# The second half of each spectrum swap, issued from ScalarE's queue

## The chip, the cores and the metric

One core of a Trainium2 chip. The metric is the device time of one execution in microseconds (us). The program uses the core's five instruction queues: TensorE (PE), VectorE (DVE), ScalarE (ACT), GpSimd (POOL) and SyncE (SP). Here SP only issues transfers (DMAs). POOL does little (iotas, memsets and seven accumulating transfers).

## What is computed

Two long convolutions over a sequence of 2048 steps and 448 channels, and a gated sum of them:

```python
g = sigmoid((x * gate_w).sum(-1, keepdims=True))   # x = A_u
a = A(x)            # kernel K[d,l] = Re sum_n C exp(dt A l) dt B, from 448 x 256 complex modes
b = B(x, k, v)      # kv = (4-tap causal conv of k) * v ; kernel ssm_k ; then times x
out = g * a + (1 - g) * b
```

Each branch is a causal convolution written as irfft(rfft(padded input) * rfft(padded kernel)) in length 4096, plus a skip term. Branch A must first make its 2048-tap kernel K from the modes.

## The kernel before

**Tiling.** The FFTs are matmuls with sine tables. The 448 channels are cut into NQG = 4 groups of 112 (4 x 28 columns). For each group H and branch, three spectra-like tiles of 128 partitions x 3584 bf16 are made in two steps: `spread` (L328, matmuls with Wc, PSUM tile ps_c) and `transform` (L340, matmuls with the table s_W, PSUM tile ps_2, shown as ps). Both are brought from PSUM to SBUF by `evac` (L728), which is a copy on ACT: in the profile "CAST zs<-ps_c" and "CAST zs<-ps" (zsK for the kernel of branch A). The tile is changed in place.

**Swap and product.** A complex product needs, beside a spectrum zs, the same spectrum with its upper and lower 64 partitions exchanged (real and imaginary parts). `swapped` (L764) makes that copy, zsS, with two transfers of 64 partitions x 3584 bf16 (448 KB each) from SBUF to SBUF. There are eight swaps: KB[0] at L852, KB[1] to KB[3] at L975, XA[0] to XA[2] at L977 and XA[3] at L1006. `products` (L399) then multiplies zsS and zs in place by the other spectrum on DVE, 2.0 us each; for XA[3], `last` (L1008) does it in quarters. Multiplying zs in place overwrites what the swap reads, so either multiply needs the swap to be through. Next `stage_a` (L374) makes ps_a from both on PE, ACT copies it to U, and `stage_b` (L387) makes ps_b.

**Work woven in between.** In `block` (L891, and KGen.block, L464), DVE builds products of exponentials for branch A's kernel (tiles kg_TQ, kg_TP, kg_P), PE multiplies them (pk, then ps_g) and ACT copies the results (kg_S, kg_KT). The tables come from `Tables.levels`: DVE makes phases (ks_ph), ACT takes sines and exponentials of them (ET, ks_mag), DVE multiplies these. ACT needs an ACT_TABLE_LOAD of 1.28 us when it changes between sine and exponential.

**Order.** Nothing runs in the order of the source. `Order` (L137) records all 6779 calls of the five engines in one list and issues them in the order of ORDER (L42), a fixed list of call numbers. Within an engine every instruction gets a dependency on the one before, so each queue runs exactly in the list's order. The two calls of a swap have neighbouring numbers (729 and 730 the first in time, 5009 and 5010 the seventh), and stand somewhere ahead of the multiply in ORDER. In the list, that is a place between calls for all engines; what it means for a queue depends on which other calls that queue holds. The line of every instruction in the profile is L149, inside `issue`, so tiles tell instructions apart. The tiles zs, zsS, U and others share six buffers (NBQ, L39).

```python
    dmae = [nc.sync, nc.scalar]
    ...
    def store(b0, n):
        for g in range(4):
            dmae[g % 2].dma_start(out4[g][:, b0:b0 + n, :], ug[g * 32:(g + 1) * 32, b0:b0 + n, :])
```

`dmae` (L714) exists already: the output is stored from SP and ACT in turn. ACT's other transfers are five small ones at the start (ldt and shift_k).

Of the kernel before, what the change touches and what calls it, by code (L numbers as in the profile page):

```python
# [690 lines left out]
def body(  # L691
# [20 lines left out]
    nc = Order(tc)  # L712
    V = nc.vector
    dmae = [nc.sync, nc.scalar]  # L714
# [25 lines left out]
    def qt(shape, name, dtype=bf16):  # L740
        return qp.tile(shape, dtype, name=name, tag="q")
# [22 lines left out]
    def swapped(zs):  # L764
        swap = qt([P, 32, 4 * NC], "zsS")
        for r in range(2):
            nc.sync.dma_start(swap[64 * r:64 * r + 64], zs[64 - 64 * r:128 - 64 * r])
        return zs, swap

    early = kgp.tile([P, 7168], i32, name="early", tag="kg_TQ")  # L770
# [79 lines left out]
    def kv_cols(H):  # L850
        return lambda c: vt[:, :, H * NC + c]
    KB[0] = swapped(KB[0])  # L852
    XB[0] = spread_in(kv_cols(0))
    transform(nc, psum, W2, XB[0], evac)
# [100 lines left out]
    def step(c, n, j):  # L955
        kind, H = n or (None, None)
        if kind == "B":
            KB[H] = spread_in(skc.pop(H))
            XB[H] = spread_in(kv_cols(H))
        elif kind == "A":  # L960
            XA[H] = spread_in(u_cols(H))
        if c:
            U = stage_a(nc, psum, qp, R, terms[c], evac)
        if kind == "B":
            transform(nc, psum, W2, KB[H], evac)
            transform(nc, psum, W2, XB[H], evac)
        elif kind == "A":
            transform(nc, psum, W2, XA[H], evac)
        if c:
            stage_b(nc, psum, G, U, epilogue(*c))  # L970
        if kind == "B" and H + 1 < NQG:
            skc[H + 1] = sk_cols(H + 1)
        block(j)
        if kind == "B":
            terms[n] = products(nc, *swapped(KB[H]), XB[H])  # L975
        elif kind == "A":
            XA[H] = swapped(XA[H])  # L977
            transform(nc, psum, W2, KA[H], evac)
            terms[n] = products(nc, *XA[H], KA[H])
# [81 lines left out]
```

## Time and profile before

| | |
|---|---|
| runs, us | 264.91, 266.36, 268.63 |
| median, us | 266.36 |
| profiled execution, us | 266.88 |
| its span, first to last instruction, us | 264.8 |
| mean granted TensorE clock | 0.942 |
| swap transfers | 16, all on SP, 448 KB each, median 4.4 us from issue to landing |
| duration of a swap's issue on SP, us | 0.46 to 2.22, median 0.56 |

Times in the profile are microseconds from the span's start. A row of a timeline is start, duration, engine, line, operation, tile written <- tiles read, shapes and count; in brackets, how long the engine had been idle and what ended that. SPq and ACTq are transfers being issued by those queues; their data arrive later ("landing"). A row of waits is who waited for whom: us in total, times, longest.

### The profile page before, as it was taken

How to read it: one execution, taken by the hardware profiler on the slowest of the kernel's cores; microseconds unless marked ns; L12 is line 12 of the kernel's file. 1: busy time of each engine (PE TensorE's matmuls, PEld its weight loads, DVE VectorE, ACT ScalarE, POOL GpSimd, SP SyncE). 2: the span in 40 equal slices, each digit the busy share in tenths (PEclk: the TensorE clock that was granted, in tenths of full speed). 3: DMA queues.
4: the chain of work that ended last, by engine and by line, in shares of the span. 5: the costliest groups of instructions: out<-in, count | busy, mean ns of one | idle time of the engine just before them, and what ended most of it. 6: DMA issues, size and time to landing. Idle time of an engine off the chain costs nothing.

```text
span 264.8 us, 12775 instructions
## 1 busy us (share of the span) xinstructions
PE 213.7 (81%) x5786; PEld 194.2 (73%) x5786; DVE 243.4 (92%) x506; ACT 226.8 (86%) x375; POOL 11.8 (4%) x46
## 2 busy tenths in 40 slices
PE   1611849799799999999899898899979998989820
PEld 1501739788688889889788788889969888979720
DVE  6599999899999999999989999989999999989950
ACT  2998789997999999999999999999999999485400
POOL 8000000000000100010100100001000100000000
PEclk9999979999999869999999999999986999999955
DMA  7999669952833702045626230423240360600087
GB/s 153 218 189 192 104 134 203 176 83 32 158 72 72 159 4 57 4 80 119 109 51 141 41 92 2 90 56 73 50 97 2 72 144 2 144 5 2 2 158 122
DMA packets 57077, 24.27 MB, mean 92 GB/s; under 512 B 52032, under 2 KB 54720, under 8 KB 57024
## 3 DMA queue, kind: packets, MB, share of 16 engines
q1 hardware_dynamic: 50752, 19.34, 38.9%
q0 software_dynamic: 1008, 3.21, 6.6%
q10 hardware_dynamic: 5264, 0.92, 2.1%
q8 instruction: 45, 0.74, 1.2%
q14 instruction: 8, 0.07, 0.1%
HBM read 7.95 MB, written 2.87 MB: 41 GB/s over the span
## 4 chain that ended last, share of the span: by engine, by line
DVE 37%; ACT 35%; PE 16%; DMA 4%; issue 3%; SPq 0%; ACTq 0%; DVEq 0%
ACT zs L149 12%; ACT zsK L149 7%; ACT ET L149 6%; DVE kg_P L149 5%; PE ps_v L149 4%; ACT U L149 4%; DVE kg_TQ L149 3%; PE ps_b L149 3%; DVE kg_TP L149 3%; DVE ET L149 3%; PE ps_c L149 3%; DVE zsS L149 3%; DVE vt L149 3%; DVE zs L149 3%; DVE sb_G L149 2%
## 5 line engine op out<-in xcount | busy, mean ns | idle before, releaser
L149 ACT CAST zs<-ps 128x896 bf16<-128x896 f32 x48 | 43.8, 944 | 1.9 <-PE ps L149 1.9
L149 ACT CAST zs<-ps_c 128x1024 bf16<-128x1024 f32 (+1 forms) x48 | 44.0, 976 | 0.5 <-PE ps_c L149 0.4
L149 PEld LDWEIGHTS <-front 128*32 128x32 bf16 (+1 forms) x496 | 19.9, 160 | 27.8 <-issue 17.3
L149 PE MATMUL pk<-kg_TP,kg_TQ 128*32 128x32 bf16 x1792 | 35.4, 241 | 0.9 <-issue 0.7
L149 PEld LDWEIGHTS <-kg_TQ 128*32 128x32 bf16 x1792 | 31.8, 160 | 3.5 <-issue 0.9
L149 PEld LDWEIGHTS <-s_W 128*128 128x128 bf16 x544 | 27.9, 98 | 7.9 <-issue 4.5
L149 PE MATMUL ps_a<-sa_R,zs 128*128 128x128 bf16 x224 | 32.0, 231 | 1.2 <-DVE zs L149 0.7
L149 PE MATMUL ps_b<-U,sb_G 128*128 128x28 bf16 x1024 | 30.8, 178 | 2.6 <-DVE U L149 1.2
L149 ACT CAST U<-ps_a 128x1024 bf16<-128x1024 f32 (+1 forms) x30 | 27.9, 962 | 5.4 <-PE ps_a L149 5.4
L149 PEld LDWEIGHTS <-sb_G 128*128 128x128 bf16 x1024 | 28.7, 98 | 4.7 <-issue 1.9
L149 PE MATMUL ps_v<-front 128*32 128x336 bf16 (+3 forms) x448 | 17.3, 319 | 17.1 <-DVE sb_offs L149 6.9
L149 PE MATMUL ps_a<-sa_R,zsS 128*128 128x128 bf16 x224 | 31.1, 227 | 0.0
L149 PEld LDWEIGHTS <-zs 128*128 128x128 bf16 x224 | 29.0, 150 | 1.9 <-DVE zs L149 0.8
L149 PEld LDWEIGHTS <-zsS 128*128 128x128 bf16 x224 | 29.4, 152 | 0.7 <-DVE zsS L149 0.4
L149 PE MATMUL ps<-zs,s_W 128*128 128x112 bf16 x384 | 27.1, 215 | 3.0 <-ACT zs L149 2.5
L149 DVE TENSOR_TENSOR kg_TP<-kg_TP,ET 128x1792 bf16<-128x1792 bf16 x23 | 24.7, 1083 | 0.5 <-ACT ET L149 0.5
L149 DVE TENSOR_TENSOR kg_TQ<-kg_TQ,ET 128x896 bf16<-128x896 bf16 (+1 forms) x36 | 24.6, 720 | 0.0
L149 ACT ACTIVATE ET<-ks_ph 128x448 bf16<-128x448 int16 x40 | 22.6, 596 | 1.8 <-DVE ks_ph L149 1.7
L149 DVE TENSOR_TENSOR kg_P<-kg_TP,ET 128x1792 bf16<-128x1792 bf16 (+1 forms) x25 | 23.3, 934 | 0.1
L149 ACT ACT_TABLE_LOAD x15 | 19.2, 1283 | 2.0 <-issue 1.8
L149 PE MATMUL ps_c<-Wc,uu 128*64 128x128 bf16 x224 | 18.7, 290 | 0.4 <-ACT zsK L149 0.2
L149 PE MATMUL ps_c<-Wc,vt 128*64 128x128 bf16 x224 | 17.2, 289 | 1.2 <-ACT zs L149 1.2
(101 smaller groups left out, 424.7 us busy)
## 6 DMA issues: line engine op xcount, KB each, us to landing
zsS<-zs SPq DMA_DIRECT2D x16, 448.0 KB, 4.4
kg_TP<-kg_P POOLq DMA_DIRECT2D x7, 448.0 KB, 4.4
vt<-in_B_v_dram SPq DMA_DIRECT2D x4, 448.0 KB, 7.5
skraw<-in_B_ssm_k_dram SPq DMA_DIRECT2D x16, 112.0 KB, 3.4
uu<-in_A_u_dram SPq DMA_DIRECT2D x4, 448.0 KB, 7.1
ks_xf<-xfd SPq DMA_DIRECT2D x3, 336.0 KB, 3.1
out_dram<-vt SPq DMA_DIRECT2D x8, 112.0 KB, 4.4
out_dram<-vt ACTq DMA_DIRECT2D x8, 112.0 KB, 4.6
```

What stands on the lines that cost most here:

```text
L149: ins = f(*args, **kw)
```

## The change

`swapped` issues its first transfer (r = 0) on SP as before and its second (r = 1) on ACT. The transfers' contents, sizes and places in ORDER stay the same.

```diff
     def swapped(zs):
         swap = qt([P, 32, 4 * NC], "zsS")
         for r in range(2):
-            nc.sync.dma_start(swap[64 * r:64 * r + 64], zs[64 - 64 * r:128 - 64 * r])
+            dmae[r].dma_start(swap[64 * r:64 * r + 64], zs[64 - 64 * r:128 - 64 * r])
         return zs, swap
```

In the built program the orders on PE, DVE and POOL are unchanged. SP loses eight transfers. ACT gains them, each at the place that its number has in ORDER among ACT's own calls:

| swap | spectrum | on ACT behind | and ahead of |
|---|---|---|---|
| 1 | KB[0] | cast zs<-ps of 66.9 us | cast zs<-ps_c of 67.67 |
| 2 | KB[1] | exponential ET<-ks_xf of 91.49 | cast zs<-ps_c of 92.00 |
| 3 | KB[2] | cast zs<-ps of 129.0 | sine ET<-ks_ph of 129.83 |
| 4 | XA[0] | exponential ET<-ks_xf of 146.5 | exponential of 146.8 |
| 5 | XA[1] | cast zs<-ps of 178.7 | sine ET<-ks_ph of 179.47 |
| 6 | KB[3] | exponential ET<-ks_xf of 199.68 | exponential of 199.97 |
| 7 | XA[2] | copy kg_KT<-ps_g of 224.09 | cast zs<-ps of 224.52 |
| 8 | XA[3] | cast zsK<-ps of 237.34 | cast zsK<-ps of 237.8 |

The times are the starts of those instructions in the trace of before.

## The prediction

> **What bounds the kernel now.** I read the page's busy lines, then the table by stretches, VectorE's (DVE) waits, and the timelines of SP, ScalarE (ACT) and DVE around each swap.
>
> ```profile
> PE 213.7 (81%) x5786; PEld 194.2 (73%) x5786; DVE 243.4 (92%) x506; ACT 226.8 (86%) x375; POOL 11.8 (4%) x46
> ```
> ```profile
> 91.50:129.00 37.50, 35.98 (x1000) 32.48 (x1003) 37.03 (x68) 36.94 (x67) 0.86 (x1) 0.92 0.33 64
> 129.00:149.00 20.00, 18.00 (x582) 16.46 (x584) 18.80 (x41) 19.32 (x37) 0.86 (x1) 1.00 0.35 74
> 149.00:178.50 29.50, 27.62 (x736) 25.24 (x730) 28.66 (x54) 29.47 (x52) 0.85 (x1) 1.00 0.29 62
> 178.50:198.60 20.10, 18.44 (x538) 16.67 (x537) 20.01 (x48) 20.07 (x34) 0.86 (x1) 0.95 0.34 73
> 198.60:220.70 22.10, 21.71 (x570) 20.10 (x568) 21.08 (x30) 21.66 (x38) 0.85 (x1) 0.89 0.31 65
> 220.70:237.90 17.20, 15.60 (x581) 14.20 (x580) 16.24 (x17) 12.54 (x20) 0.00 (x0) 1.00 0.25 57
> ```
> The columns are the stretch, its length, then busy time of PE, weight loads, DVE, ACT, POOL. From 91.5 to 237.9 us DVE idles 0.47+1.20+0.84+0.09+1.02+0.96 = 4.6 us out of 146.4, and ACT is full until 220. Two in-order engines without slack hand work to each other: a DVE stall is hardly ever absorbed.
>
> DVE's waits, longest first:
> ```profile
> DVE front L149 <- DMA scratch<-in_B_shift_k_dram: 3.1, 1, 3.1
> DVE ks_ph L149 <- ACT ET L149: 1.9, 2, 1.1
> ...
> DVE zsS L149 <- ACT zsK L149: 0.6, 2, 0.4
> ```
> Only the start-up wait is for a DMA. No multiply ever waits for a swap: all sixteen swap transfers are hidden, so landing them sooner buys nothing.
>
> The place where I expect most, on SP, ACT and DVE:
> ```profile
> 212.28 1.10 SPq L149 DMA_DIRECT2D zsS<-zs  x2
> ```
> ```profile
> 222.65 0.53 ACT L149 CAST kg_S<-pk 128x448 bf16<-128x448 f32 x1
> 223.14 0.91 ACT L149 CAST zs<-ps 128x896 bf16<-128x896 f32 x1
> 224.09 0.53 ACT L149 CAST kg_KT<-ps_g 128x448 bf16<-128x448 f32 x1
> 224.52 0.91 ACT L149 CAST zs<-ps 128x896 bf16<-128x896 f32 x1
> ```
> ```profile
> 220.76 2.02 DVE L149 TENSOR_TENSOR zsS<-zsS,zsK 128x3584 bf16<-128x3584 bf16 x1 [0.39 <-ACT zsK L149]
> ```
> SP issues both halves at 212.28, far ahead of the multiply at 220.76. In the changed kernel's own order the second half stands on ACT behind the kg_KT copy of 224.09 and ahead of the cast of 224.52: after the multiply that needs it.
>
> Does ACT's queue reach a transfer early? The start-up is the one spot with a DMA behind an ACT instruction that waits:
> ```profile
> 4.42 0.20 ACT L149 ACTIVATE scratch<-ldt 112x4 bf16<-112x4 bf16 x1 [1.36 <-DMA ldt<-in_A_log_dt_dram]
> 4.43 1.35 ACTq L149 DMA_DIRECT2D scratch<-in_B_shift_k_dram  x3
> ```
> The first of these three transfers waits for nothing, yet goes out 0.01 us after the ACTIVATE ahead gets its data. It does not wait for that ACTIVATE's end (4.62), but it does not overtake its wait either. So a transfer on ACT leaves when the last ACT instruction ahead of it has what it waits for.
>
> **Landing price.** Swap issues land after 4.0/4.4/6.7 us (least, median, most; the tile view of zsS). The late ones are second halves queued behind their first; one issued alone, as here, should be near the short end: 4.2 us, between 4.0 and 4.4; 6.7 is the far bound.
>
> **Part 1: eight second halves leave SP.** SP is rid of 8 x 0.56 us (median issue) and of some waits; it idles for most of the span, and the skraw and ks_xf loads behind it move up 0.6 us but nobody waits for them. Worth 0. A faster landing is worth 0 too, as above.
>
> **Part 2: ACT's time.** Issues on ACT's queue cost 0.42 (ldt) to 0.56 us. Behind a 0.9 us cast they are hidden, since the queue works while the engine does; behind the 0.39, 0.53 and 0.55 us instructions of the second, seventh and eighth swap some 0.1 to 0.2 us shows, and there ACT will soon be waiting for DVE anyway. I take 0; the bounds are 0 and 8 x 0.56 = 4.5 us.
>
> **Part 3: the added wait on DVE.** A multiply needs both halves: zsS is written by them, and zs may not be overwritten until both were read. Per swap: the ACT row ahead of the transfer, that time + 4.2, the multiply's start now, and the difference.
> - First: cast at 66.9 (second of the pair 66.09 to 67.81), lands 71.1; multiply 72.94. On time, 0.
> - Second: ET exponential at 91.49, kept until then by the table load of 90.20 + 1.28; lands 95.7; multiply 91.74. **4.0 late.**
> - Third: cast at 129.0 (second of 128.06 to 129.93), 133.2; multiply 129.78. **3.4.**
> - Fourth: between 144.64 (a table load ends and six exponentials and casts can be queued) and 146.5 (the last of them starts); lands 148.8 to 150.7; multiply 149.12: -0.3 to 1.6. I take **0.5**, as little behind that table load waits for anybody.
> - Fifth: cast at 178.7, 182.9; multiply 178.52. **4.4.**
> - Sixth: cast at 198.89 (the exponential behind it waits for nothing), 203.1; multiply 198.59. **4.5.**
> - Seventh: 224.09, 228.3; multiply 220.76. **7.5.**
> - Eighth: zsK cast at 237.34, 241.5; multiply 237.90. **3.6.**
>
> Sum 27.9 us. Behind each stalled multiply the whole DVE queue waits: ks_ph phases that ACT turns into ET tables, kg_TP/kg_TQ that PE multiplies, the products that PE's ps_a needs. So ACT becomes late as well, and with it the next swap's transfer; that is why the stalls add. Two things are taken off. DVE's own idle time of 4.6 us can absorb lateness once. And where ACT has a lead over DVE it is less late at the next transfer: after the second swap the exponentials at 98.34 use a kg_TP sum that ended at 97.16, a lead of 1.2, of which the idle time already counts 0.3: 0.9. Elsewhere the lead is nearly nil: the PE waits for "DVE zs" at 224.78, right behind the product. Net 27.9 - 4.6 - 0.9 = **22.4 us**.
>
> The profiled execution took 266.88 us (span 264.8 and 2.1 around it; the median of the runs is 266.36). 266.9 + 22.4 = 289.3; I say **289 us**.
>
> Bounds: least, if lateness never reached ACT, so that stalls did not add: the largest alone, 7.5, gives 274. Most: nothing absorbed and every issue paid, 27.9 + 4.5 gives 299. The value is nearer the upper end, as ACT and DVE are both full.
>
> [...]
>
> **Rivals.**
> 1. *ACT's queue overtakes (not slower).* If a transfer on ACT passed instructions that still wait, it would leave as soon as its own data and buffer are there, which is when SP issues it now: 212.28 + 0.5 for the seventh swap, not 224.09. All seven would be on time as today: 266.9. It decides only if such passing happens, against which the rows at 4.42 and 4.43 speak. [...] The start-up rows show a transfer held back with a single waiting instruction ahead.
> 2. *Stalls do not add up.* ACT keeps going while DVE waits, so each transfer leaves near its old time and DVE's lateness covers the next stall: 274 to 280. For it: ACT's table work has leads of about 1 us here and there. Against: ACT's full rows and its many waits for DVE and, through PE, for products.
> 3. *More than counted.* Landings take 6.7 us as the slowest now do: seven late swaps x 2.5 us more, 266.9 + 22.4 + 17.5 = 307. Against: nothing is queued ahead of a half that leaves 10 us after the other.
> 4. *The swap truly gets faster.* Both halves leave together and DVE gains: at most 8 x 0.56 = 4.5 us, 262. Against: no multiply waits for a swap today.
>
> **How the numbers follow.** Forecast with adding stalls 0.83; rival 1, 0.04; rival 2, 0.06; rival 3, 0.06; rival 4, 0.01. The likeliest is 289. If ACT found its lead of 1.2 again behind each of the five late swaps that follow the second (6.0) and all landings took 4.0 (7 x 0.2), the sum would be 15.0 and the time 281.9; the range starts at 280, the edge of rival 2, and ends at 299, the bound with every issue paid and nothing absorbed. It leaves out under 2 in 10. About 2% is what a measurement of this kernel tells from no change: faster 0.01, within 2% 0.04, slower 0.95.
>
> **What would show it.** DVE's waits should have new entries, zs and zsS waiting for the DMA zsS<-zs, seven of them and over 20 us in all, the longest about 7 us at the seventh swap. Issues should read eight on SPq and eight on ACTq, the latter just behind the ACT rows named, landing in 4.0 to 4.4 us. DVE's busy time should stay at 243 us and its share fall to about 84%. PE should run the same 5786 matmuls with more gaps, ps_a's above all. I am wrong if ACTq's swap issues come earlier than the ACT instruction ahead gets its data, or if ACT is found on time at each next transfer although DVE was late.

## The result and the profile after

| | before | changed |
|---|---|---|
| median, us | 266.07 | 296.0 |
| range, us (4 runs each) | 264.91 to 268.63 | 295.28 to 296.6 |
| profiled execution, us (span) | 266.88 (264.8) | 295.92 (294.1) |
| mean granted TensorE clock in it | 0.942 | 0.913 |

The ratio is 1.110, 95% interval 1.105 to 1.114: slower by 11%, 30 us. The forecast was 289, from 280 to 299.

The busy line of the changed kernel's page; each entry is busy time, share of the span and count:

```profile
PE 220.0 (75%) x5786; PEld 199.8 (68%) x5786; DVE 243.7 (83%) x506; ACT 227.8 (77%) x375; POOL 11.8 (4%) x46
```

DVE and ACT do the same work in about the same busy time as before (243.4 and 226.8 us then). PE needs 220.0 us instead of 213.7 for the same 5786 matmuls, at the lower granted clock of the table above. For DVE, the 29 us are waiting. Who makes DVE wait, longest first (us in total, times, longest):

```profile
DVE zsS L149 <- DMA zsS<-zs: 12.4, 3, 7.8
DVE zsS L149 <- PE ps L149: 4.6, 1, 4.6
DVE zs L149 <- DMA zsS<-zs: 4.4, 1, 4.4
DVE zs L149 <- ACT kg_S L149: 4.1, 1, 4.1
DVE zsS L149 <- ACT uu L149: 3.9, 1, 3.9
...
DVE kg_KT L149 <- PE ps_g L149: 2.2, 1, 2.2
...
DVE ks_ph L149 <- ACT ET L149: 0.2, 1, 0.2
```

Before, not one of these waits was for a swap. Now the five upper rows, 29.4 us over seven multiplies, are. Three of them name PE or ACT as the releaser, which is the profile's guess among several semaphores: those multiplies (191.17, 137.85 and 215.06 us) start 4.0 to 4.9 us after an ACT issue of a swap; of the four that name the DMA, three do so 4.0 to 4.1 us after one, and the multiply at 96.39 starts 6.2 us after.

The seventh swap in the changed kernel, on SP's queue, on ACT and its queue, then on DVE:

```profile
228.74 0.46 SPq L149 DMA_DIRECT2D zsS<-zs  x1
```
```profile
239.62 0.91 ACT L149 CAST zs<-ps 128x896 bf16<-128x896 f32 x1
240.57 0.53 ACT L149 CAST kg_KT<-ps_g 128x448 bf16<-128x448 f32 x1
240.63 0.47 ACTq L149 DMA_DIRECT2D zsS<-zs  x1
241.14 0.91 ACT L149 CAST zs<-ps 128x896 bf16<-128x896 f32 x1
```
```profile
244.61 2.03 DVE L149 TENSOR_TENSOR zsS<-zsS,zsK 128x3584 bf16<-128x3584 bf16 x1 [7.76 <-DMA zsS<-zs]
```

SP issued the first half at 228.74. The second leaves 0.06 us after the kg_KT copy ahead of it starts, 11.9 us later, and the multiply begins 4.0 us after that. ACT itself loses nothing: the next cast follows at 241.14.

### The profile page after: what moved, and what is told of

Its sections match the earlier page's. It is cut to its first block, busy times and chain, and to the rows that moved or that the text cites. A ratio compares the mean times of both kernels' runs of the same rounds, so it can differ in the third digit from the quotient of the medians.

```text
span 294.1 us, 12780 instructions
## 1 busy us (share of the span) xinstructions
PE 220.0 (75%) x5786; PEld 199.8 (68%) x5786; DVE 243.7 (83%) x506; ACT 227.8 (77%) x375; POOL 11.8 (4%) x46
## 3 DMA queue, kind: packets, MB, share of 16 engines
q1 hardware_dynamic: 50112, 15.67, 29.7%
## 5 line engine op out<-in xcount | busy, mean ns | idle before, releaser
L149 PE MATMUL ps_a<-sa_R,zs 128*128 128x128 bf16 x224 | 37.2, 254 | 18.7 <-DVE zs L149 18.1
L149 PEld LDWEIGHTS <-zs 128*128 128x128 bf16 x224 | 31.1, 154 | 19.7 <-DVE zs L149 18.7
L149 ACT CAST zs<-ps_c 128x1024 bf16<-128x1024 f32 (+1 forms) x48 | 43.3, 957 | 0.3 <-PE ps_c L149 0.3
L149 ACT CAST U<-ps_a 128x1024 bf16<-128x1024 f32 (+1 forms) x30 | 27.1, 929 | 20.4 <-PE ps_a L149 20.3
L149 PEld LDWEIGHTS <-front 128*32 128x32 bf16 (+1 forms) x496 | 20.9, 158 | 26.6 <-issue 15.8
L149 PE MATMUL ps_a<-sa_R,zsS 128*128 128x128 bf16 x224 | 36.4, 251 | 2.0 <-DVE zsS L149 2.0
L149 PEld LDWEIGHTS <-zsS 128*128 128x128 bf16 x224 | 31.5, 155 | 3.0 <-DVE zsS L149 2.6
L149 PE MATMUL ps_v<-front 128*32 128x224 bf16 (+3 forms) x448 | 18.5, 335 | 15.7 <-DVE front L149 6.9
L149 DVE TENSOR_TENSOR zsS<-zsS,zsK 128x896 bf16<-128x896 bf16 (+1 forms) x7 | 8.5, 1223 | 17.0 <-DMA zsS<-zs 12.4
```

What stands on the lines that cost most here:

```text
L149: ins = f(*args, **kw)
```

## The experiments

Two theories. *Place*: a transfer on ACT leaves when ACT's queue has come to its place in the list; DVE's stalls are the whole loss, and they add. Rival, *queue*: an issue from ACT, or a second queue of transfers, costs by itself wherever it stands. A second question is what makes the loss larger than forecast. Each run was timed against the kernel before on the same chip (267.16 us in the first four, 266.94 in the last three).

**1. The same queue, an earlier place.** Eight numbers of ORDER moved; all else as changed (in short, as the list itself is one long string):

```diff
-ORDER: second halves 730, 1833, 3306, 2455, 3928, 5854, 5010, 5954 at their old places
+ORDER: 730 behind 1346, 1833 behind 2902, 3306 behind 4173, 2455 behind 3419,
+       3928 behind 2875, 5854 behind 5459, 5010 behind 5503, 5954 behind 5219
```

> All eight second halves stay on ACT, but each stands earlier in the list, right behind the first ACT call that starts 0.2 us or more after SP's issue of that swap in the trace of before (65.17, 84.59, 123.24, 141.75, 168.57, 190.11, 212.59, 226.06 us). Theory place (a transfer on ACT leaves when ACT's queue has come to its place, and the stalls of DVE are all of the loss): it leaves about as early as SP's half, lands before every multiply, DVE waits for no swap; 266 to 268 us. Rival queue (issuing from ACT costs by itself: ACT's time, or two queues that get into each other's way): the same eight issues, so still about 290 us or more.

Measured: 269.9 us, ratio 1.0105 (1.0055 to 1.0154). DVE's waits:

```profile
DVE front L152 <- DMA scratch<-in_B_shift_k_dram: 3.4, 1, 3.4
DVE ks_ph L152 <- ACT ET L152: 3.2, 2, 2.1
...
DVE kg_TP L152 <- ACT ET L152: 1.0, 1, 1.0
```

No swap is waited for any more, so 26 of the 30 us are gone with the same eight issues on ACT. The time lies 2 us above what I expected. DVE waits longer for ET tables than before (3.2 + 1.0 against 1.9 + 0.5 us), and ACT now has eight issues of about 0.47 us in its queue. That these are the cause is not shown: in the trace of run 2, where ACT issues no swap, the ks_ph wait is 2.9 us as well. The cause of these 2 us stays open. The run bounds what issuing on ACT costs: 1%, not 11%.

**2. A queue with little in it, the old place.**

```diff
-            dmae[r].dma_start(swap[64 * r:64 * r + 64], zs[64 - 64 * r:128 - 64 * r])
+            [nc.sync, nc.gpsimd][r].dma_start(swap[64 * r:64 * r + 64], zs[64 - 64 * r:128 - 64 * r])
```

> The list is as in the changed kernel, but the second half goes out on POOL's queue, which holds only seven accumulating transfers besides. Theory place: what stands ahead on POOL is done early, so the swap leaves in time although its number stands at the same late place of the list; 266 to 269 us. Rival queue, in the form that transfers from two queues slow each other: 285 us or more. If POOL's issue itself took long, landings would be 1 to 2 us later than from SP, which the multiplies can bear.

Measured: 267.58 us, ratio 1.0025 (0.9999 to 1.005): the same as before. POOL's first half left at 65.0 us and its last at 226.4; SP's left at 64.5 and 226.1. So on this queue the late place in the list cost nothing, and neither did a second queue of transfers (267.58 against 267.16 us). Nor did it bring the pair home sooner when both halves left close together: in this run the halves of both queues landed 4.0 to 7.6 us after their issue (median 5.7; before, 4.0 to 6.7, median 4.4), and ACT's in run 1 after 5.1 to 6.5 (median 6.2), where the second halves on SP's queue before took 5.7 to 6.7. So even at a good place the second queue shortened no swap. With run 1 this settles *place*: it takes ACT's full queue and the late place together.

**3. Only the seventh swap on ACT.** `swapped` counts its calls (in the source's order, XA[2] is the sixth) and uses ACT in that one alone (shortened):

```diff
+        count.append(1)
         for r in range(2):
-            dmae[r].dma_start(...)
+            dmae[r * (len(count) in (6,))].dma_start(...)
```

> Only the seventh swap (XA[2]) has its second half on ACT. Theory place: one stall of about 7.5 us at its multiply, 0.4 to 1 of it absorbed by DVE's own idle time and some more given back through a longer kg_KT wait as in the changed kernel; 272 to 276 us, middle 274. Rival queue: an eighth of the loss of 30, so 270 us; the stall at the seventh multiply would not be 7 us.

Measured: 275.4 us, ratio 1.0332 (1.0279 to 1.0385): 8.2 us from one transfer.

```profile
DVE zsS L149 <- DMA zsS<-zs: 7.8, 1, 7.8
...
DVE kg_KT L149 <- PE ps_g L149: 2.2, 1, 2.2
```

The stall is the 7.8 us of the changed kernel, and the longer kg_KT wait comes with it (0.6 before).

**4. Both halves on ACT.**

```diff
-            dmae[r].dma_start(...)
+            nc.scalar.dma_start(...)
```

> Both halves of every swap go out on ACT, at their places in the list. Theory place: the departure is as in the changed kernel, but now two transfers queue behind each other, and the pair is complete 5.7 to 6.7 us after the first issue, not 4.0; at seven swaps with a stall that is 1.7 to 2.5 us each on top, since nothing absorbs it: 296 + 12 to 18 = 308 to 314 us. Rival queue: the loss per ACT issue doubles, 296 + 30 = 326 us.

Measured: 310.07 us, ratio 1.162 (1.157 to 1.167), within 308 to 314 and far from 326. DVE's waits for swaps have grown to 24.3 + 13.3 us, and 4.6 more under PE's name. Doubling ACT's issues did not double the loss; the first halves too now stand in ACT's queue (sixteen issues, from 66.9 to 276.9 us), and landings take up to 7.7 us, where the changed kernel's take up to 6.7.

**5. Only the second swap on ACT** (`in (2,)` in the edit of run 3), 200 us of program behind it:

> Only the second swap (KB[1]) has its second half on ACT: one stall of about 4.4 us at its multiply, with the whole rest of the program behind it to make up for it. Theory absorption (as my prediction had it: DVE's 4.6 us of idle time take up lateness once): nearly all is made up, 266 to 268 us. Theory pass-through (most of that idle time is DVE waiting for ACT or PE, which are late as well, so little is made up; in the changed kernel only 0.3 and 1.1 of the idle rows that follow went away): 1.5 made up, 269.5 to 271 us.

Measured: 270.48 us, ratio 1.0126 (1.0094 to 1.0159): *pass-through*. The multiply and DVE's largest waits:

```profile
95.90 2.03 DVE L149 TENSOR_TENSOR zs<-zs 128x3584 bf16<-128x3584 bf16 x1 [4.25 <-DMA zsS<-zs]
```
```profile
DVE zs L149 <- DMA zsS<-zs: 4.2, 1, 4.2
DVE front L149 <- DMA scratch<-in_B_shift_k_dram: 3.3, 1, 3.3
DVE ks_ph L149 <- ACT ET L149: 1.9, 2, 1.1
```

The ks_ph waits for ACT stay at 1.9 us, as before: ACT was late by as much as DVE, so this idle time absorbed nothing. All of DVE's idle rows over 0.15 us from the first swap on, other than the stall, sum to 3.6 us here and to 4.1 before. Of 4.2 us, 3.5 reach the end.

**6. Only the eighth swap on ACT** (`in (8,)`):

> Only the eighth swap (XA[3]) has its second half on ACT. In the changed kernel the eighth multiply lost 5.1 us more than the seventh, of which 3.7 is the stall itself and 1.6 a longer wait of the kg_KT cast for PE ahead of it. If that wait is an aftermath of the seventh stall, as the run with the seventh alone says (2.2 us there too), it stays at 0.6 here and the time is 266.5 + 3.6 = 270 us, 269.5 to 271. If the eighth swap causes it, 272 us.

Measured: 271.12 us, ratio 1.0159 (1.0129 to 1.0188), 0.1 above the range given. The stall is 4.1 us and kg_KT waits 0.6: the longer kg_KT wait is an aftermath of the seventh stall.

**7. All but the seventh** (`in (1, 2, 3, 4, 5, 7, 8)`):

> All swaps but the seventh have their second half on ACT. If stalls add: 296.0 less the 8.2 that the seventh alone cost, 287.8 us, 286.5 to 289. If stalls overlap (ACT keeps its time while DVE waits), the other swaps would cost more without the seventh: 291 us or more. If the throttle or ACT issues as such set the loss, seven eighths of 30, 292 us.

Measured: 286.71 us, ratio 1.0724 (1.0687 to 1.0761), 19.8 us above its own before. With the 8.2 of run 3 that is 28.0, against 29.9 for all eight at once. The stalls add; if they overlapped, the two parts would sum to more than the whole.

**Where the longer kg_KT wait comes from.** The changed kernel around the seventh multiply of 244.61 us (columns: stretch, length, busy PE, PEld, DVE, ACT, POOL, then PEclk, DMA share and GB/s):

```profile
242.90:253.00 10.10, 4.37 (x50) 3.90 (x51) 8.32 (x9) 1.46 (x2) 0.00 (x0) 0.50 0.31 66
253.10:258.00 4.90, 4.90 (x178) 4.53 (x179) 4.84 (x5) 2.13 (x3) 0.00 (x0) 1.00 0.02 3
```

The first 40 ps_a matmuls that use its product, from the start of the first to the end of the last (columns: stretch, length, busy PE with the matmuls in it, DVE, ACT, then PEclk, DMA share and GB/s): in the changed kernel, in run 3, in run 7 without that stall, and before.

```profile
248.63:253.66 5.03, 4.36 (x40) 0.00 (x0) 1.49 (x2) 0.56 0.45 94
```
```profile
231.05:236.13 5.08, 4.41 (x40) 0.00 (x0) 1.55 (x2) 0.55 0.79 180
```
```profile
242.35:245.80 3.45, 2.98 (x40) 0.00 (x0) 1.49 (x2) 1.00 0.51 104
```
```profile
224.78:228.22 3.44, 2.98 (x40) 0.00 (x0) 1.48 (x2) 1.00 0.51 107
```
```profile
262.52 0.63 DVE L149 CAST kg_KT<-ps_g 128x448 bf16<-128x448 f32 x1 [2.16 <-PE ps_g L149]
```

While DVE stalls, PE runs out of work: its last matmul ends at 240.53 us and the next starts at 248.63. The granted clock is 0.50 from about 242.8 to 253.1 and 1.00 after that. The 40 matmuls, with a few of ps_g between them, take 5.0 us instead of 3.4. Everything else in this chain keeps its length: the first ps_a starts 4.0 us after the multiply in both kernels, and from the last of the 40 to the kg_KT cast (at 262.52, and at 237.07 before) it is 8.9 us in both. So the stall is paid a second time, 1.6 us, as slower matmuls. (Of run 3's 7.8 and 1.6 us, 8.2 reach the end: 0.4 of the stall stood there before as a wait for zsK, and where the rest went is open.) Run 3, with the same stall, has 0.50 at this place too (227 to 235 us, then 0.95 from 235 to 241); without it the clock there is 1.00 (before, 220.7 to 238; run 6, 219 to 241; run 7, 238.3 to 256). In the changed kernel the half clock set in 2.3 us after PE's last matmul and ended 4.4 us after the next began. An idle PE is not all that goes with it: before, the clock is 0.50 from 90.8 to 97.5 us, though PE was busy for 3.14 of the 3.41 us ahead of that and for 6.68 of these 6.70. No run changed the clock by itself.

## Why the prediction was right, and where it was off

**What bounds the kernel, and what the change is worth.** Right. Two full in-order engines (DVE busy for 92% and ACT for 86% of the span before); SP's lighter load bought nothing (run 2, 267.58 against 267.16 us), and nobody had waited for a landing.

**When a transfer leaves ACT.** Right. Seven of the eight left within 0.3 us of the start of the last instruction ahead that had to wait for its input, as the start-up rows said: an instruction ahead must have had what it waits for, and need not be finished (the seventh left at 240.63 us, and the copy ahead of it ran from 240.57 to 241.10). The second swap left sooner than I reckoned:

```profile
89.79 0.61 ACT L149 ACTIVATE ET<-ks_ph 128x448 bf16<-128x448 int16 x1
90.18 0.47 ACTq L149 DMA_DIRECT2D zsS<-zs  x1
90.42 1.28 ACT L149 ACT_TABLE_LOAD   x1
91.72 0.39 ACT L149 ACTIVATE ET<-ks_xf 128x224 bf16<-128x224 f32 x1
```

It passed a table load and an exponential that stood ahead. DVE's multiply that reads ET had ended at 90.14, so the exponential had what it waits for. I had let the table load hold the transfer. Rival 1 (a transfer passes waiting instructions) fell: at the seventh swap it was held for 11.9 us with its data there and left right behind the row ahead of it, and seven swaps stalled.

**The landing price.** 4.2 us was right for half of the swaps (median 4.0, least 3.8), and too little where other transfers ran beside: 6.7 us at the first swap, next to skraw loads, and 6.1 at the second, next to POOL's accumulating transfer of 88.78 (issue at 90.18, multiply at 96.39). At the third and fifth, again next to a transfer of POOL (134.32 and 186.78), the multiply started 4.9 and 4.5 us after the issue. At the second swap this made up for the early start, so that its 4.0 came near by luck; the first, reckoned on time, was 0.6 late.

**The stalls, swap by swap** (DVE's idle time just before the multiply; the sum is of unrounded times):

| swap | 1 | 2 | 3 | 4 | 5 | 6 | 7 | 8 | sum |
|---|---|---|---|---|---|---|---|---|---|
| forecast, us | 0 | 4.0 | 3.4 | 0.5 | 4.4 | 4.5 | 7.5 | 3.6 | 27.9 |
| measured, us | 0.6 | 4.4 | 4.1 | 0.9 | 4.6 | 3.9 | 7.8 | 3.7 | 29.9 |

The first swap's 0.6 us stands under "ACT zs" in the profile; its half landed at 73.28 and the multiply began at 73.36.

**What is taken off.** This is the step that was mis-sized. I took 5.5 us off: "DVE's own idle time of 4.6 us can absorb lateness once", and a lead of 0.9. DVE's idle rows over 0.15 us from the first swap on, other than these stalls, sum to 4.1 us before and to 3.9 in the changed kernel: 0.2 us net. Part of it did go (ks_ph's waits for ACT fell from 1.9 to 0.2), and as much came back elsewhere (kg_KT from 0.6 to 2.2). Run 5 says why idle time is no reserve: most of it is DVE waiting for ACT or PE, which a DVE stall makes late too. So 29.9 - 0.2 gives 29.7 us, and the execution took 29.0 more (295.92 against 266.88), where I had 22.4. The stalls themselves were 2.0 us longer than reckoned, which adds to the same side. The range held because its upper end was reckoned with nothing absorbed.

**Rivals 2 to 4.** Stalls that do not add: refuted by runs 3 and 7. Landings of 6.7 us throughout, and a faster swap: not seen.

## What to carry to other kernels

A transfer inherits the queue that issues it. On POOL's queue, which held little else, its place in the program's order hardly mattered (267.58 against 267.16 us); on the queue of a busy compute engine, here ACT, it left only after everything listed ahead had had its inputs, at the seventh swap 11.9 us after the half on SP (with all eight there, 296.0 against 266.07 us), so move the place along with the transfer or pick an empty queue. Ask first whether anybody waits for the transfer: no multiply did, so there was nothing to win. And when several in-order engines are full, count every stall in full, without taking off the idle time in the rows: here 29.9 us of stalls cost 29.0, for that idle time was mostly waiting for engines which the same stall made late.

## What the runs showed of the hardware that I had not expected

A transfer on ACT's queue passed a table load that had not begun: it was issued at 90.18 us and the load ran from 90.42. The seventh stall on DVE came with half of PE's granted clock (0.50 for some 10 us), and the slower matmuls added 1.6 us of waiting to its 7.8. ACT's 448 KB transfers in the changed kernel landed after 3.8 to 4.0 us where no other transfer was issued near them, and after 4.8 to 6.7 beside transfers of SP or POOL. Two halves of a swap that left close together from two queues were no sooner there than from one (median of 6.2 us for the second half in run 1, against 5.7 to 6.7 before; median of 5.7 us for all halves in run 2, against 4.4 before).
